# Talking-heads attention with a squared-ReLU FFN: a fixed TensorE order with FFN, AV and transposes as filler, AV heads in paired column tiles, full token tiles, fold on GpSimd

## The chip, the cores and the metric

One core of one Trainium2 chip. Time is device microseconds of one execution. The kernel before takes 1078.01 us (median of four runs beside those of the changed kernel, 1072.89 to 1087.81). A profile is one execution of its own, so its span (1088.0 us for the kernel before, the profile of the slowest of the four runs) differs a little from the median. A "visit" below is one stay of TensorE in a tiling of its array, with entering and leaving: *row tiles* where the two heads of QK read partitions 0 to 63 and 64 to 127, *column tiles* where the two heads of AV write PSUM partitions 0 to 63 and 64 to 127 with 64 stationary columns each.

## The reference, cut to what matters

```python
# q, k, v: (8, 12, 448, 64); w_pre, w_post: (12, 12); w_in: (768, 2048); w_out: (2048, 768)
scores = scale * q @ k.T                                # QK
scores = einsum('bhij,hg->bgij', scores, w_pre)         # pre: mixes the 12 heads
attn   = softmax(scores, axis=-1)                       # exp, row sum, division
attn   = einsum('bhij,hg->bgij', attn, w_post)          # post: mixes the heads again
x      = attn @ v                                       # AV, then tokens x 768
out    = relu(x @ w_in) ** 2 @ w_out                    # first and second FFN matmul
```

The head mixes need the 12 heads of a query on the partition axis. Both kernels handle a chunk of 10 queries, 120 rows of (query, head), 45 chunks to a batch. A chunk goes: QK into PSUM, copy to `stage`, a DMA that relays `stage` (query rows) into `dring` (query and head rows), `pre`, exp on ScalarE with its row sum, reciprocal on VectorE, *fold* (post's matrix scaled by the reciprocals), `post`, copy to `a2t`.

## The kernel before

Each batch's work is a list of tasks with estimates, and a greedy planner decides the order on every engine by start time and priority. AV runs once all 45 chunks of a batch are done. It splits the 448 keys into row blocks of 128, 128, 128 and 64, and takes the two heads of a pair one after the other:

```python
for p in range(NPAIR):
    for kk in range(2):                       # the two heads of a pair
        kh = 2 * p + kk
        for jb in range(NJT):                 # 4 blocks of keys
            nrj = min(128, S - jb * 128)      # 128, 128, 128, 64
            last = eng.matmul(
                psV[kk * 64:kk * 64 + 64, hcol0:hcol0 + ncol],
                vbv[0:nrj, pb, jb, kh, :],            # stationary, 64 columns
                a2t[0:nrj, jb, kh, 0:nch_h * CH],     # moving, 450 columns
                start=(jb == 0), stop=(jb == NJT - 1))
    ...
# first FFN: one PSUM bank (psH), 16 groups of 6 matmuls, relu and square on VectorE
# second FFN: four token tiles a batch (128, 128, 128, 64), 32 matmuls each, in one go
for hh, (f0, fw) in enumerate(FSPL):
    for t16 in range(NFFT):
        last = eng.matmul(psA[0:M, hh, 0:fw], h2t[:, t16, tt*128:tt*128+M],
                          w_out_sb[:, t16, f0:f0+fw], ...)
# fold, on VectorE
i1 = eng.reciprocal(rinv[:, psl, :], rowsum[:, psl, :])
selfsync(DVE, eng, i1)
return eng.tensor_scalar(wk2s[:, ws, :], wk2b[:, :], rinv[:, psl, :], None, op0=ALU.mult)
```

The softmax here doesn't subtract the row's maximum and nothing guards it: scores larger than these inputs give would overflow.

## Time and profile before

| | kernel before |
|---|---|
| median time | 1078.01 us |
| span of the profile | 1088.0 us |
| TensorE busy | 866.5 us (80%) |
| VectorE, ScalarE busy | 495.5 and 435.4 us |
| mean granted TensorE clock | 0.786 |
| from one batch's first post to the next one's (batches 1 to 7) | 119.6 us |

The page's totals, and its strip of 40 equal slices. A digit is the busy share of a slice in tenths; PEclk is the granted clock in tenths of full speed.

```profile
PE 866.5 (80%) x4744; PEld 413.6 (38%) x4744; DVE 495.5 (46%) x1377; ACT 435.4 (40%) x1061; POOL 98.0 (9%) x108
...
PE   1356678897889798788989798888889798848777
...
ACT  0345544634354515643353615543454425430001
...
PEclk9555669895998759995798759996989569965559
```

TensorE is the busiest engine, but much of this time is at half clock. The stage table of the kernel before says when (columns: stretch, its length, busy time and instructions of each engine, granted clock, DMA share, GB/s):

```profile
140.00:160.00 20.00, 14.51 (x59) 5.62 (x59) 7.62 (x19) 7.36 (x18) 0.00 (x0) 0.64 0.23 39
...
460.00:480.00 20.00, 18.88 (x131) 11.85 (x130) 3.86 (x15) 7.67 (x21) 0.00 (x0) 1.00 0.29 81
...
500.00:520.00 20.00, 18.81 (x49) 5.44 (x50) 4.68 (x9) 4.43 (x7) 0.00 (x0) 0.50 0.17 34
...
1000.00:1020.00 20.00, 15.69 (x39) 4.58 (x38) 5.32 (x10) 0.00 (x0) 0.00 (x0) 0.50 0.00 1
```

The four rows are batch 0's attention, a second FFN stage (VectorE and ScalarE have little to do), an AV stage, and the end (batch 7's first FFN). Two of them run at clock 0.50, and in the AV row TensorE is nevertheless busy 18.8 of 20 us.

TensorE's timeline of the kernel before, first a mixed stage at full clock, then AV (start, length, what, how many):

```profile
427.06 0.40 PE L368 MATMUL psA<-ktp,qtp 64*120 64x448 bf16 x2
427.39 0.40 PE L427 MATMUL psP<-dring,wk 120*120 120x448 bf16 x1
427.85 1.31 PE L560 MATMUL psH<-xt,w_in_sb 128*128 128x448 bf16 x6
429.09 0.40 PE L368 MATMUL psA<-ktp,qtp 64*120 64x448 bf16 x2
...
502.23 3.62 PE L514 MATMUL psV<-a2t,vbv 128*64 128x450 bf16 x8
505.78 0.63 PE L368 MATMUL psA<-ktp,qtp 64*120 64x448 bf16 x2
506.57 3.62 PE L514 MATMUL psV<-a2t,vbv 128*64 128x450 bf16 x8 [0.16 <-DVE xt L535]
```

Starts, not lengths, give the cost: a QK pair is recorded with 0.40 us, but the next matmul starts 0.33 us after it. A first-FFN group takes 1.24 us to a following QK and 1.14 us where `pre` follows. An AV group (one pair of heads) lasts 3.62 us, and QK follows after 3.55; the groups recur every 4.34 us.

### The profile page before, as it was taken

The page shows a single profiled execution, that of the slowest core. Times are in us where ns is not written, and L with a number is a line of the kernel's source. Part 1 is how long each engine was busy: PE and PEld are TensorE (multiplying, and loading weights), DVE is VectorE, ACT ScalarE, POOL GpSimd, SP SyncE. Part 2 cuts the span into 40 slices and gives each one's busy share as a digit, 9 for nine tenths or more (in the row PEclk, how much of TensorE's full clock was granted, in tenths as well). Part 3 has the DMA queues.
Part 4 walks back from the last instruction along what each step waited for, and adds up shares of the span by engine and source line. Part 5 has one row for each costly group of instructions (what it writes and reads, how often), then busy time and mean ns, then how long its engine had stood idle before and what let it go on. Part 6 is the DMA issues. An engine that isn't in the chain of part 4 may idle for free.

```text
span 1088.0 us, 13619 instructions
## 1 busy us (share of the span) xinstructions
PE 866.5 (80%) x4744; PEld 413.6 (38%) x4744; DVE 495.5 (46%) x1377; ACT 435.4 (40%) x1061; POOL 98.0 (9%) x108
## 2 busy tenths in 40 slices
PE   1356678897889798788989798888889798848777
PEld 1122323463345424452345424452446234522224
DVE  1134536815573527643582527543763447331320
ACT  0345544634354515643353615543454425430001
POOL 8500201002100201011100200000100000000000
PEclk9555669895998759995798759996989569965559
DMA  9996916329532917348532907331633213220001
GB/s 94 183 204 79 101 32 78 53 65 112 64 55 52 114 22 86 58 84 80 70 55 64 106 16 86 58 80 29 81 49 82 44 36 57 62 48 0 1 0 51
DMA packets 184643, 73.25 MB, mean 67 GB/s; under 512 B 135168, under 2 KB 180224, under 8 KB 184576
## 3 DMA queue, kind: packets, MB, share of 16 engines
q0 software_dynamic: 133408, 22.81, 29.3%
q1 hardware_dynamic: 51168, 49.57, 22.8%
q8 instruction: 38, 0.62, 0.2%
q14 instruction: 29, 0.24, 0.1%
HBM read 45.62 MB, written 11.01 MB: 52 GB/s over the span
## 4 chain that ended last, share of the span: by engine, by line
PE 36%; DVE 13%; ACT 4%; issue 4%; DMA 3%; SPq 0%; DVEq 0%; ACTq 0%
PE psA L607 12%; PE psV L514 10%; PE psH L560 9%; DVE h1t L577 4%; DMA dring<-stage 3%; PE psQ L467 2%; DVE a2t L491 2%; DVE wk2s L455 2%; ACT pring L439 2%; DVE xt L535 2%; PE psP L427 2%; ACT osb L627 1%; DVE rinv L453 1%; PE psA L368 1%; DVE stage L389 1%
## 5 line engine op out<-in xcount | busy, mean ns | idle before, releaser
L439 ACT ACTIVATE pring<-psP 120x448 bf16<-120x448 f32 x360 | 193.8, 541 | 230.7 <-PE psP L427 149.8
L467 PE MATMUL psQ<-wk2s,pring 120*128 120x120 bf16 x1440 | 148.7, 242 | 86.6 <-DVE wk2s L455 70.8
L560 PE MATMUL psH<-xt,w_in_sb 128*128 128x448 bf16 x768 | 187.0, 385 | 27.5 <-DVE h1t L577 18.2
L607 PE MATMUL psA<-w_out_sb,h2t 128*128 128x384 bf16 (+1 forms) x1024 | 179.0, 335 | 10.9 <-ACT osb L627 9.2
L388 ACT ACTIVATE stage<-psA 120x896 bf16<-120x896 f32 (+1 forms) x128 | 117.3, 917 | 139.6 <-PE psA L368 138.3
L427 PE MATMUL psP<-dring,wk 120*120 120x448 bf16 x360 | 148.1, 436 | 30.8 <-DMA dring<-stage 24.9
L467 PEld LDWEIGHTS psQ<-wk2s,pring 120*128 120x128 bf16 x1440 | 105.2, 109 | 158.3 <-ACT pring L439 77.6
L514 PE MATMUL psV<-a2t,vbv 128*64 128x450 bf16 (+1 forms) x384 | 153.6, 524 | 12.5 <-DVE xt L535 11.8
L453 DVE RECIPROCAL rinv<-rowsum 120x1 f32<-120x1 f32 x360 | 57.3, 159 | 226.4 <-ACT pring L439 184.9
L491 DVE CAST a2t<-psQ 128x480 bf16<-128x480 f32 x180 | 117.6, 654 | 70.5 <-PE psQ L467 70.4
L607 PEld LDWEIGHTS psA<-w_out_sb,h2t 128*128 128x128 bf16 (+1 forms) x1024 | 103.1, 103 | 81.8 <-ACT osb L627 14.6
L490 ACT ACTIVATE a2t<-psQ 128x480 bf16<-128x480 f32 x180 | 103.3, 574 | 53.3 <-PE psQ L467 53.2
L368 PE MATMUL psA<-ktp,qtp 64*120 64x448 bf16 (+1 forms) x384 | 99.2, 513 | 24.4 <-ACT stage L388 10.3
L627 ACT ACTIVATE osb<-psA 128x768 f32<-128x768 f32 (+1 forms) x32 | 25.9, 809 | 224.9 <-PE psA L607 224.9
L577 DVE TENSOR_SCALAR h1t<-psH 128x448 bf16<-128x448 f32 x128 | 79.7, 623 | 76.4 <-PE psH L560 74.6
L560 PEld LDWEIGHTS psH<-xt,w_in_sb 128*128 128x128 bf16 x768 | 69.7, 104 | 117.9 <-DVE h1t L577 55.8
L455 DVE TENSOR_SCALAR wk2s<-wk2b,rinv 120x120 bf16<-120x120 bf16 x360 | 98.3, 273 | 12.7
L535 DVE CAST xt<-psV 128x448 bf16<-128x448 f32 x48 | 30.0, 625 | 134.5 <-PE psV L514 134.5
L514 PEld LDWEIGHTS psV<-a2t,vbv 128*64 128x64 bf16 (+1 forms) x384 | 42.8, 135 | 123.6 <-issue 90.6
L427 PEld LDWEIGHTS psP<-dring,wk 120*120 120x120 bf16 x360 | 53.8, 152 | 77.2 <-DMA dring<-stage 34.6
L389 DVE CAST stage<-psA 120x896 bf16<-120x896 f32 (+1 forms) x64 | 69.4, 1084 | 14.6 <-PE psA L368 14.3
L439 ACT ACTIVATION_READ_ACCUMULATOR pring<-psP 120x1 f32 x360 | 72.0, 200 | 0.0
(26 smaller groups left out, 281.2 us busy)
## 6 DMA issues: line engine op xcount, KB each, us to landing
dring<-stage SPq DMA_DIRECT2D x352, 105.0 KB
out_dram<-osb SPq DMA_DIRECT2D x24, 384.0 KB, 2.3
qraw<-in_q_dram POOLq DMA_DIRECT2D x32, 168.0 KB, 6.5
kraw<-in_k_dram POOLq DMA_DIRECT2D x32, 168.0 KB, 6.8
vbv<-in_v_dram POOLq DMA_DIRECT2D x24, 192.0 KB, 6.4
w_in_sb<-in_moe_w_in_dram POOLq DMA_DIRECT2D x1, 3072.0 KB, 19.7
w_out_sb<-in_moe_w_out_dram POOLq DMA_DIRECT2D x1, 3072.0 KB, 40.8
out_dram<-osb SPq DMA_DIRECT2D x8, 192.0 KB, 2.6
```

The source lines that it names most:

```text
L368: last = eng.matmul(psA[0:nr, par, 0:S], qtp[r0:r0 + 64, p, T * IT:T * IT + nr], ktp[r0:r0 + 64, p, 0:S], start=True, stop=True,)
L388: return eng.activation(o, i_, AF.Copy)
L427: return eng.matmul(psP[0:NR, pbank, 0:S], wk1[:, :], dring[:, slot, 0:S], start=True, stop=True)
L439: return eng.activation(pring[:, psl, 0:S], psP[0:NR, pbank, 0:S], AF.Exp, accum_out=rowsum[:, psl, :],)
L455: return eng.tensor_scalar(wk2s[:, ws, :], wk2b[:, :], rinv[:, psl, :], None, op0=ALU.mult)
L467: last = eng.matmul(psQ[0:128, qbank, jb * NR:(jb + 1) * NR], pring[:, psl, jb * 128:jb * 128 + 128], wk2s[:, ws, :], start=True, stop=True,)
L490: return eng.activation(dst, src, AF.Copy)
L491: return eng.tensor_copy(dst, src)
L514: last = eng.matmul(psV[kk * 64:kk * 64 + 64, hcol0:hcol0 + ncol], vbv[0:nrj, pb, jb, kh, :], a2t[0:nrj, jb, kh, 0:nch_h * CH], start=(jb ...
L560: last = eng.matmul(psH[0:128, 0:S], w_in_sb[:, ft, t16 * 128:(t16 + 1) * 128], xt[:, pb, ft, 0:S], start=(ft == 0), stop=(ft == NFT - 1),)
L577: return eng.tensor_scalar(h1t[:, hslot, 0:S], psH[0:128, 0:S], 0.0, None, op0=ALU.max)
L607: last = eng.matmul(psA[0:M, hh, 0:fw], h2t[:, t16, tt * 128:tt * 128 + M], w_out_sb[:, t16, f0:f0 + fw], start=(t16 == 0), stop=(t16 == N ...
```

## The change

The kernel is rewritten around one idea: TensorE's order is fixed by the program, chunk by chunk, and everything that is not the chain of chunks becomes filler in small pieces.

```diff
+        def window(b):                         # filler of batch b's window
+            head = weave(units_AV(b - 1, 1), late_f2, 2)      # AV, second half of batch b-1
+            f1 = units_F1(b - 1, ...)                         # first FFN, 2 pieces of 3 matmuls
+            ts = units_T(b + 1) if b + 1 < B else []          # next batch's transposes
+            body = weave(f1, ts, 2)
+            body += mark(lambda: emit_load_qk(b + 2))
+            body += units_F2(b - 1, ...)                      # second FFN, 4 pieces of 4 matmuls
+            tail = units_AV(b, 0)                             # AV, first half (26 chunks) of batch b
...
+            if 0 <= s + LP < NG:
+                emit_pre(s + LP)                # pre runs 3 chunks ahead of post
...
+                    while openg or queue:       # filler, paced by its share of the work left
+                        if w and owed < w / 2:
+                            break
...
+        emit_load_qk(0); emit_load_v(0); emit_load_w()        # the loads' order in the program
+        for p in range(NP):
+            emit_T(0, p)
+            emit_QK(*qk_order[p])
+        emit_load_qk(1)
```

AV now splits the keys into four blocks of 112 rows, and its two heads alternate; there are two halves of 260 and 188 columns:

```diff
-                                for kk in range(2):
-                                    for jb in range(NJT):
-                                        nrj = min(128, S - jb * 128)
+                for r in range(RJ):             # 4 blocks of 112 keys
+                    for kk in range(2):
+                        r_ = eng.matmul(psF[kk * 64:kk * 64 + 64, bank, 0:n],
+                                        vraw[:, 2 * p + kk, r, :],
+                                        a2t[half][:, r, 2 * p + kk, 0:n], ...)
```

The 64-token rest of an even batch shares a second-FFN tile with that of the odd batch after it (28 full tiles instead of 32). Fold runs on GpSimd, and the squares too, except batch 7's. Evictions go to ScalarE or VectorE as the planner's model finds either free; the transposes are made as half-width tiles (768 instead of 384); q, k and v are loaded in rows of 4 tokens, so with a quarter of the pieces.

## The prediction

> **What bounds the kernel now.** Totals show TensorE busy 866.5 of 1088 us, VectorE 495.5, ScalarE 435.4, mean granted clock 0.786. The stage table (20 us windows) shows three regimes:
> - Opening (to 245 us, when batch 0's FFN ends): from 40 to 160 us TensorE is busy 7 to 15 of each 20 us at clock 0.50 to 0.64; nothing fills the attention's waits.
> - Steady, about 119 us a batch (second FFN matmuls recur at 340, 460, 580). AV alone (500 to 527) runs at clock 0.50 although TensorE is busy 18.8 of 20 us: 64 columns a matmul, the two heads of a pair in sequence. The second matmuls run with ScalarE and VectorE nearly idle; attention after them waits for wk2s and psA.
> - Ending (960 to 1088): batch 7 alone, mostly clock 0.50, each first matmul group waiting for its relu.
>
> So TensorE's order and clock bound the time.
>
> **TensorE at full clock**, start to start in the timeline: first FFN group 1.14 us, second 0.162 us per matmul, pre 0.19, post 0.21 (4 matmuls), QK pair 0.33 plus 0.10 before it. Two concurrent row tiles need 0.19, so entering and leaving costs about 0.24. The Trainium skill (TensorEngine Tiling (Array Packing), Key Properties) says that changing the tiling mode drains TensorE; this agrees.
>
> **What the change does there.**
> - AV: 384 matmuls of 450 columns in sequence (27 us a batch at half clock) become paired column tiles. The skill (TensorE: Matmul & The Clock Gate, Part 3) says such tiles run concurrently; here only QK's row tiles show it. Estimate 7.6 us a batch with switches, at full clock.
> - Second FFN: 28 full tiles for 32, 166 to 146 us.
> - Transposes: 768 half-width for 384; estimate 38 us with switches, some 18 more.
> - FFN, AV and transposes fill between pre, QK and post: TensorE should not idle, the clock stay near 1.0 (mixed windows at 420 to 460 show 1.00).
>
> Sum after, at full clock (estimate): pre 68, post 76, QK 83, AV 61, transposes 38, FFN 146 + 146: about 618 us.
>
> **Other engines.** Fold leaves VectorE (98 us) for GpSimd, as do squares (50) except batch 7's. Evictions split flexibly: from the measured durations at most 460 us each on ScalarE and VectorE, below TensorE. GpSimd: estimate 300 to 350 us, off the path with three chunks of lookahead (some 5 us). Q, k, v loads get four times fewer packets. The relayout DMAs (38 MB) stay, with slack.
>
> **Predicted time.** Opening 25 us until chunks flow; batch 0, limited by ScalarE/VectorE and the weight loads' DMA, about 55; windows 1 to 7 about 80 each (78 of TensorE work plus waits), 560; ending 30. Total about 670 us: steady periods save some 40 each, the opening 85, the ending 95. Range 620 to 745. Faster by over 2%: 0.97; within 2%: 0.02; slower: 0.01.
>
> **What shows it right or wrong.** Mean clock over 0.9; TensorE busy over 90% from 100 us on; period near 80 us; AV matmuls starting in pairs, about 1.3 us per head pair over both halves; batch 0 chunks every 1.2 us; GpSimd not high among TensorE's releasers; ending under 40 us.
>
> **What would make it wrong.** (1) Mode switches cost over 0.24 us, or come more often, with QK, AV and transposes scattered: period 90 or more. (2) Column tiles don't overlap: 7 us a period. (3) Fold late behind squares or DMA issues on GpSimd: posts wait, and the fixed order has no way around. (4) Weight loads crowd the opening's relayouts and the clock stays 0.5: 30 to 50 us. (5) Evictions late, two psF banks serving four stages. If everything overlaps better: 620.

## The result, and the profile after

| | before | after |
|---|---|---|
| median time | 1078.01 us | 721.18 us (720.45 to 723.25, 4 runs) |
| span of the profile | 1088.0 us | 718.5 us |
| TensorE busy | 866.5 us (80%) | 629.5 us (88%) |
| mean granted clock | 0.786 | 0.985 |
| first post of batch 0 | 48.2 us | 64.0 us |
| first post of batch 1 | 170.7 us | 144.5 us |
| batch to batch, batches 1 to 7 | 119.6 us | 75.3 us |
| from batch 7's first post to the end | 199.4 us | 122.3 us |

The ratio is 0.6682 (95% interval 0.6646 to 0.6718). Ratios are the mean time of one kernel's fast runs over that of the other's of the same rounds, so not quite the ratio of the medians quoted. Executions over 1.5% slower than the fastest of the same kernel are left out of the means. Where I compare experiments with the changed kernel, I give medians in us. The kernel before scattered in the later jobs (1046 to 1095 us in the last, where eight of its eleven runs count as slow) and several verdicts against it are marked unclear for that reason; the changed kernel and its variants stay within about 1%.

The page's totals and strip after:

```profile
PE 629.5 (88%) x5576; PEld 368.6 (51%) x5576; DVE 380.7 (53%) x946; ACT 488.9 (68%) x1129; POOL 287.0 (40%) x566
...
PE   3314779987889999999999999999999999999996
...
ACT  4314660897878967788778867887788676866510
```

From the thirteenth slice on (216 us) TensorE is full. The stage table after, cut at the windows of the batches (a window runs from a batch's first post to the next one's); columns as before:

```profile
0.00:64.00 64.00, 14.97 (x137) 7.69 (x138) 7.71 (x12) 16.70 (x25) 15.39 (x31) 1.00 1.02 173
64.00:144.00 80.00, 66.83 (x558) 40.81 (x556) 47.89 (x116) 48.07 (x118) 27.48 (x61) 0.91 0.38 74
144.00:208.00 64.00, 52.27 (x578) 33.40 (x578) 44.56 (x116) 53.42 (x137) 28.20 (x67) 0.95 0.63 122
...
288.00:362.00 74.00, 73.89 (x669) 41.52 (x665) 45.37 (x111) 60.61 (x140) 36.15 (x68) 1.00 0.57 109
362.00:442.00 80.00, 78.24 (x691) 44.13 (x685) 45.71 (x111) 62.26 (x142) 36.14 (x68) 1.00 0.53 109
...
682.00:718.00 36.00, 29.31 (x252) 18.97 (x250) 12.22 (x35) 3.84 (x11) 2.75 (x5) 0.99 0.12 45
```

Windows alternate between 74 and 80 us, because even batches bring three second-FFN tiles and odd ones four; they run in the window of the next batch. TensorE is busy all but 2 us of them, at clock 1.00. The first 64 us are another matter: TensorE is busy 15 us. Their clock of 1.00 is not a measurement: the trace records no change of clock before 75.5 us, and the views put 1.00 where nothing is recorded. By the lengths of its matmuls (0.58 us for `post` up to 74.8 us, 0.39 at 75.5) TensorE ran at half clock until then.

TensorE's timeline after, in a full window (the parts answer to the lines shown of before):

```profile
337.46 0.38 PE L489 MATMUL psQ<-wk2s,pring 120*128 120x120 bf16 x4
337.76 0.63 PE L521 MATMUL psF<-a2t,vraw 112*64 112x260 bf16 x8
338.33 0.40 PE L444 MATMUL psP<-dring,wk 120*120 120x448 bf16 x1
...
342.42 0.40 PE L377 MATMUL psA<-ktp,qtp 64*120 64x448 bf16 x2
342.75 0.38 PE L489 MATMUL psQ<-wk2s,pring 120*128 120x120 bf16 x4
342.97 0.35 PE L444 MATMUL psP<-dring,wk 120*120 120x448 bf16 x1
```

An AV group of 260 columns takes 0.57 us to the next start, plus some 0.09 before it (post alone takes 0.21, here 0.30); with the 188-column half that is about 1.2 us a pair of heads instead of 4.34. And the timeline of the opening:

```profile
39.58 0.63 PE L377 MATMUL psA<-ktp,qtp 64*120 64x448 bf16 x2
41.13 0.63 PE L444 MATMUL psP<-dring,wk 120*120 120x448 bf16 x1 [0.92 <-DMA dring<-stage]
63.08 0.59 PE L336 MATMUL psF<-ident,qraw 112*64 112x112 bf16 x8 [21.32 <-DMA kraw<-in_k_dram]
63.45 0.59 PE L336 MATMUL psF<-ident,kraw 112*64 112x112 bf16 x8
63.97 0.58 PE L489 MATMUL psQ<-wk2s,pring 120*128 120x120 bf16 x4
```

Four chunks have been through `pre` and exp by 42 us, but the first `post` comes at 64 us. Ahead of it, in the fixed order, stand the transposes of batch **1**, and they wait 21.32 us for batch 1's k. That load was issued at 24.4 us; the whole of `w_in` and `w_out` had been issued from the same queue at 14 us. The list of DMA issues has the k loads of one head pair at 4.1 us to landing (median) and this one at 38.6.

### The profile page after: what moved, and what is told of

Its sections match the earlier page's. It is cut to its first block, busy times and chain, and to the rows that moved or that the text cites. A ratio compares the mean times of both kernels' runs of the same rounds, so it can differ in the third digit from the quotient of the medians.

```text
span 718.5 us, 14744 instructions
## 1 busy us (share of the span) xinstructions
PE 629.5 (88%) x5576; PEld 368.6 (51%) x5576; DVE 380.7 (53%) x946; ACT 488.9 (68%) x1129; POOL 287.0 (40%) x566
## 4 chain that ended last, share of the span: by engine, by line
PE 81%; DMA 7%; ACT 4%; DVE 4%; POOL 2%; issue 1%; SPq 0%; POOLq 0%
PE psF L625 21%; PE psF L562 20%; PE psQ L489 13%; PE psP L444 9%; PE psA L377 9%; PE psF L521 6%; DMA kraw<-in_k_dram 6%; PE psF L336 4%; DMA dring<-stage 2%; ACT pring L454 1%; DVE a2t L220 1%; ACT stage L219 1%; POOL h2t L597 1%; DVE qtp L220 1%; ACT a2t L219 1%
## 5 line engine op out<-in xcount | busy, mean ns | idle before, releaser
L469 POOL TENSOR_SCALAR wk2s<-wk2b,rinv 120x120 bf16<-120x120 bf16 x360 | 131.0, 365 | 305.2 <-DVE rinv L463 302.3
L220 DVE CAST a2t<-psQ 112x480 bf16<-112x480 f32 x221 | 144.5, 656 | 99.5 <-PE psQ L489 95.6
L562 PE MATMUL psF<-xt,w_in_sb 128*128 128x448 bf16 (+2 forms) x960 | 187.0, 316 | 5.1 <-DVE ktp L220 3.2
L625 PE MATMUL psF<-w_out_sb,h2t 128*128 128x384 bf16 x896 | 177.2, 325 | 9.0 <-POOL h2t L597 7.4
L597 POOL TENSOR_TENSOR h2t<-h1t 128x448 bf16<-128x448 bf16 (+2 forms) x128 | 107.3, 839 | 37.0 <-DVE h1t L588 17.6
L625 PEld LDWEIGHTS psF<-w_out_sb,h2t 128*128 128x128 bf16 x896 | 82.0, 98 | 54.1 <-POOL h2t L597 9.3
L562 PEld LDWEIGHTS psF<-xt,w_in_sb 128*128 128x128 bf16 x960 | 84.1, 99 | 47.8 <-DVE ktp L220 5.6
L377 PE MATMUL psA<-ktp,qtp 64*120 64x448 bf16 (+1 forms) x384 | 80.5, 416 | 26.3 <-ACT stage L219 13.6
L219 ACT ACTIVATE a2t<-psQ 112x480 bf16<-112x480 f32 x139 | 80.0, 575 | 28.8 <-PE psQ L489 24.9
L377 PEld LDWEIGHTS psA<-ktp,qtp 64*120 64x120 bf16 (+1 forms) x384 | 25.0, 127 | 81.8 <-issue 32.0
L521 PE MATMUL psF<-a2t,vraw 112*64 112x260 bf16 (+1 forms) x768 | 53.5, 264 | 1.7 <-DVE a2t L220 0.7
L588 DVE TENSOR_SCALAR h1t<-psF 128x448 bf16<-128x448 f32 (+2 forms) x89 | 43.8, 492 | 10.6 <-PE psF L562 9.0
```

Source lines behind the costliest of these rows:

```text
L219: return eng.activation(o, i_, AF.Copy)
L220: return eng.tensor_copy(o, i_)
L377: r_ = eng.matmul(psA[0:nr, par, 0:S], qtp[r0:r0 + 64, pb, p, T * IT:T * IT + nr], ktp[r0:r0 + 64, pb, p, 0:S], start=True, stop=True,)
L469: return eng.tensor_scalar(wk2s[:, ws, :], wk2b[:, :, :].rearrange("p a b -> p (a b)"), rinv[:, ps, :], 1.0, op0=ALU.mult, op1=ALU.mult)
L521: r_ = eng.matmul(psF[kk * 64:kk * 64 + 64, bank, 0:n], vraw[:, 2 * p + kk, r, :], a2t[half][:, r, 2 * p + kk, 0:n], start=(r == 0), stop= ...
L562: r_ = eng.matmul(psF[:, bank, 0:n], w_in_sb[:, ft, t16 * 128:(t16 + 1) * 128], xt[:, ft, c0:c1], start=(ft == 0), stop=(ft == NFT - 1),)
```

## The experiments

Twelve kernels were run; all gave correct results. Those named b change the kernel before, the others the changed kernel (721.18 us).

### e1: weights after batch 1's loads, first try

```diff
         emit_load_v(0)
-        emit_load_w()
         ...
         emit_load_qk(1)
+        emit_load_w()
```

> The changed kernel (721 us) with one edit: the FFN weight loads are issued after batch 1's q and k loads instead of before them. Theory A (the opening lost to the load order: TensorE stands 21 us at batch 1's first transpose because its k tile is queued behind 12.6 MB of weights): that wait goes, chunk 0's post starts near 40 us instead of 64, and the run takes 700 to 708 us; not the whole 21 us, because the relayouts of batch 0 now compete with the weights for longer. Rival (the opening is bound by TensorE's own chain of transposes, evictions and half clock, the load wait only hides it): under 5 us gained.

Measured 721.61 us (716.67 to 724.08), with the same wait of 21.5 us. This decides nothing: the instruction lists of all engines, GpSimd's included, turned out to be identical to those of the changed kernel. So e1 is a second sample of it, in another job. The planner orders GpSimd's tasks by readiness and priority, and the weights were ready earlier and ranked higher. Moving a line in a program whose order is made by a planner is not an edit; look at the instruction list of the engine before running.

### e2: batch 1's transposes later in the order, loads unchanged

```diff
             ts = units_T(b + 1) if b + 1 < B else []
-            body = weave(f1, ts, 2)
+            if b == 0: late_t.extend(ts + mark(lambda: emit_load_qk(2)))
+            else:      body = weave(f1, ts, 2)
...
+            if b == 0 and c == 14:
+                queue, owed = late_t, 0.0
```

> The changed kernel with the loads in their old order, but batch 1's transposes put into TensorE's order from chunk 14 of batch 0 on instead of ahead of chunk 0's post. Theory A with the fixed order as its second half (the late load stops TensorE only because the order puts its transposes first): posts start near 42 us instead of 64 while the weights still load, time 700 to 708 us. If the load alone mattered and the order did not: no gain, TensorE waits for the same DMA later.

Measured 707.75 us (705.49 to 709.12), 13 us less. The first post comes at 41.5 us, and its timeline reads:

```profile
41.12 0.63 PE L444 MATMUL psP<-dring,wk 120*120 120x448 bf16 x1 [0.91 <-DMA dring<-stage]
41.54 0.61 PE L489 MATMUL psQ<-wk2s,pring 120*128 120x120 bf16 x4
43.23 0.63 PE L444 MATMUL psP<-dring,wk 120*120 120x448 bf16 x1 [1.08 <-DMA dring<-stage]
...
70.78 0.59 PE L336 MATMUL psF<-ident,qraw 112*64 112x112 bf16 x8 [6.01 <-DMA kraw<-in_k_dram]
```

So the wait came of the late load and the order together: with the order alone changed, the wait ahead of the first post is gone. The 22 us gained at the first post shrink to 13 because the chunks now come every 2.1 us, at the pace at which their relayouts pass beside the weight loads (each `pre` waits for its DMA), and chunk 14's transposes still wait 6 us for k.

### e8: the loads' order really changed

```diff
-            last["w_in"] = plan.add("ldwin", POOL, fn_in, [qk_tasks[(0, H - 1)]], ..., -300.0, ...)
+            last["w_in"] = plan.add("ldwin", POOL, fn_in, [last["T"]], ..., 600.0, ...)
             # the same for w_out; emit_load_w() after emit_load_qk(1) as in e1
```

> e1 repeated with the order really changed: the edit of e1 left GpSimd's queue as it was, because its own planner sorts loads by priority and readiness; here the weight loads wait for the last transpose of batch 0 and rank behind batch 1's q and k. TensorE's order is that of the changed kernel. Theory A (load order): the 21 us wait for batch 1's k tile shrinks to under 3 us, posts start near 41 us, but the relayouts now run beside the weights until about 95 us at 2.1 us a chunk, and the first FFN group may wait for w_in a little: 703 to 712 us. Rival (own chain and half clock): over 716 us.

Measured 710.74 us (707.82 to 711.82). The wait for k is gone, the first post comes at 42.9 us, and again only half of the gain stays. In e2 and in e8 alike, TensorE reaches AV of batch 0's first 26 chunks at 92.2 us, against 104.3 in the changed kernel. Two opposite cures end at the same moment, which would fit a limit in the bytes of the DMA queues, but no run isolates it. The stage table of e8 shows them full up to 70 us (last two columns: DMA share, which counts packet time and passes 1.0 here, and GB/s):

```profile
40.00:50.00 10.00, 5.50 (x60) 3.41 (x60) 3.75 (x7) 2.77 (x6) 0.73 (x2) 1.00 1.08 221
50.00:60.00 10.00, 8.01 (x73) 4.88 (x74) 4.46 (x10) 7.19 (x14) 2.65 (x4) 1.00 1.13 222
60.00:70.00 10.00, 5.82 (x31) 2.77 (x29) 5.09 (x14) 5.05 (x13) 2.29 (x7) 1.00 1.21 219
```

From 70 to 90 us the share is 0.77. In e2 it falls to 0.69 and 0.28 from 60 to 80 us, and the 6 us wait for k lies there; so the queues are not full all the way to 92 us in either run.

The Trainium skill says that DMAs from the SP, ACT and POOL queues all run on the same 16 DMA engines and interleave (Trainium Kernel Development and Optimization, Key Constraints). This agrees: in e2 a chunk's relayout from the SP queue passes every 2.1 us beside the weights from the POOL queue; once `w_out` has landed at 55.4 us, chunks come every 1.25 us on average until the wait at 64.4 us.

### e3: AV's two heads one after the other

```diff
-                for r in range(RJ):
-                    for kk in range(2):
+                for kk in range(2):
+                    for r in range(RJ):
```

> The changed kernel with the two heads of a pair run one after the other in AV (all four row groups of one head, then of the other), nothing else changed. Column tiles overlap theory: the matmuls no longer start in pairs, AV costs 0.73 us more per head pair over both halves, 48 pairs, 35 us in all: 750 to 760 us, clock still over 0.95 because other work surrounds AV. Rival 1 (tiles don't overlap, it was the weaving that saved the time): no change. Rival 2 (unpaired AV pulls the clock to half as it did in the kernel before): 800 us or more.

Measured 722.05 us (715.34 to 723.59): no change, where I expected 35 us more. Rival 1, no overlap at all, is not the reason either, for an AV group still takes 0.57 to 0.58 us, and eight matmuls of 260 columns in sequence would take 8 x 0.11 us (0.11 is the step between starts within one head):

```profile
332.03 0.64 PE L521 MATMUL psF<-a2t,vraw 112*64 112x260 bf16 x8
332.61 0.40 PE L444 MATMUL psP<-dring,wk 120*120 120x448 bf16 x1
```

The single starts in that group, from the trace, are 332.033, .047, .168, .182, .279, .292, .390 and .403: still in pairs, 13 to 14 ns apart (4 ns in the changed kernel). So the two column tiles overlap **even though the program gives four matmuls of one head first**. The trace doesn't name the tile of a matmul, but two of one head, which add into the same PSUM cells, are 0.11 us apart; the partner in each pair must be the other head's.

Then why did the heads not overlap in the kernel before, in the same order? Its single starts in one group are 502.234, 502.613, 502.987, 503.499, 504.009, 504.386, 504.761 and 505.272. Steps are 0.375 us, but 0.51 into and out of the fourth matmul, the one with only 64 rows. A new theory: the 64-row block, a different tiling in the middle, keeps the heads apart. The next two runs test it on the kernel before.

### b2: the kernel before with four blocks of 112 keys, heads in sequence

```diff
-                    nrj = min(128, S - jt * 128)
-                    off = b * H * S * D + jt * 128 * D
+                    nrj = S // NJT                                   # 112, in the load of v
+                    off = b * H * S * D + jt * nrj * D
-                                pring[:, psl, jb * 128:jb * 128 + 128],
+                                pring[:, psl, jb * 112:jb * 112 + 128],
-                                        nrj = min(128, S - jb * 128)
+                                        nrj = S // NJT               # in AV
```

> The kernel before, with only the split of the 448 keys changed: four blocks of 112 rows instead of 128, 128, 128 and 64, in the loads of v, post's slices and AV; the two heads still in sequence. Theory U: without the 64-row block no tiling change stands between the heads and they overlap by themselves, as they did in e3: an AV group takes 1.9 to 2.2 us instead of 3.6 at the half clock, 48 groups, 70 to 80 us less: 995 to 1015 us. Rival (heads in sequence do not overlap in this kernel; e3 overlapped for another reason): no change, 1070 to 1085 us.

Measured 1016.3 us (1014.63 to 1020.26), just above the range, and 43 us under the median of the three fast runs of the kernel before in that job (1059.75). The ratio is 0.9634 (0.9534 to 0.9733), unclear for their scatter; the timeline is clear. The group has become:

```profile
482.58 1.72 PE L514 MATMUL psV<-a2t,vbv 112*64 112x450 bf16 x8
485.04 1.72 PE L514 MATMUL psV<-a2t,vbv 112*64 112x450 bf16 x8 [0.18 <-DVE xt L535]
```

The period of the groups falls from 4.34 to 2.46 us without any change of order, and that of the batches from 119.6 to 110.0 us.

### b1: the kernel before with the heads alternating, blocks unchanged

```diff
-                                for kk in range(2):
-                                    kh = 2 * p + kk
-                                    for jb in range(NJT):
-                                        nrj = min(128, S - jb * 128)
+                                for jb in range(NJT):
+                                    nrj = min(128, S - jb * 128)
+                                    for kk in range(2):
+                                        kh = 2 * p + kk
```

> The kernel before, with only AV's loop order changed: row block outside, the two heads inside, so that heads alternate as in the changed kernel. Row blocks stay 128, 128, 128 and 64. Theory U (what keeps the heads apart in the kernel before is the 64-row block, which changes the tiling, not the order): with the order changed too, the three 128-row blocks start in pairs and the 64-row pair once more, so an AV group takes about 2.4 us instead of 3.6 at the half clock, 48 groups, 55 to 60 us: 1015 to 1030 us. Rival (order alone decides and nothing else): groups of about 1.9 us.

Measured 1026.28 us (1022.65 to 1030.98), inside the range (ratio 0.9725, 0.9619 to 0.9831, unclear for the same reason), but the group takes 1.85 us, not the 2.4 I expected:

```profile
487.68 1.85 PE L514 MATMUL psV<-a2t,vbv 128*64 128x450 bf16 x8
```

So either edit is enough alone: alternate the heads, and the 64-row pair comes last and costs 0.13 us against b2; or cut even blocks, and the order no longer matters. What separates the heads in the kernel before is the combination, the odd block standing between them. In both runs an AV matmul still lasts 0.58 us, the half-clock length, and the granted clock from 480 to 500 us is 0.50: pairing did not lift the clock of a stage that runs by itself with gaps.

### e4: filler in one block

```diff
-                        if w and owed < w / 2:
+                        if False:
                             break
```

> The changed kernel with the pacing taken out: each window's filler (AV, first and second FFN matmuls, transposes) is emitted in one block at the start of its window, then the 45 chunks of attention follow. Theory (interleaving is what hides the chunks' chain of exp, reciprocal, fold and evictions): a window becomes about 45 us of dense FFN with ScalarE idle plus 45 to 60 us of attention with TensorE under 70% busy, 95 to 105 us instead of 77: 830 to 900 us. Rival (the gain came from cheaper TensorE work alone, order is secondary): under 750 us.

Measured 872.09 us (867.67 to 874.77), 151 us more than the changed kernel, inside the range. The same TensorE work falls apart into stages again. Two rows of the stage table of this run, the block of filler and the 45 chunks after it:

```profile
218.00:274.00 56.00, 50.05 (x375) 26.43 (x376) 13.30 (x20) 14.54 (x33) 20.54 (x26) 0.96 0.41 73
274.00:323.00 49.00, 38.92 (x322) 22.24 (x320) 36.39 (x90) 41.96 (x114) 15.58 (x43) 0.90 0.42 92
```

In the first ScalarE is busy 14.5 of 56 us; in the second it is busy 42 of 49, nearly the limit, and TensorE 39. The windows become 94 to 106 us. The two stages load different engines, and interleaving is what lets them share the time.

### e5: fold back on VectorE

```diff
-            t_fold = add("fold%d_%d" % (b, c), POOL, fn_fold, ..., {POOL: (350.0, 450.0)}, ...)
+            t_fold = add("fold%d_%d" % (b, c), DVE, fn_fold, ..., {DVE: (200.0, 280.0)}, ...)
```

> The changed kernel with fold back on VectorE (0.27 us each, 98 us in all). Theory (TensorE's work bounds the steady windows, 100% busy; VectorE has room at 53% busy): within 1%, 715 to 728 us, VectorE about 65% busy. Rival (moving fold off VectorE is part of the gain): over 735 us.

Measured 721.24 us (719.9 to 722.65): the same. VectorE rises to 62% busy and has room. Moving fold to GpSimd is harmless and buys nothing here.

```profile
PE 628.8 (88%) x5576; PEld 367.1 (51%) x5576; DVE 448.1 (62%) x1263; ACT 500.3 (70%) x1172; POOL 157.7 (22%) x206
```

### e6: every QK pair twice

```diff
-                for par in range(2):
+                for par in (0, 1, 0, 1):
```

> The changed kernel with every QK pair issued twice in a row (the second overwrites the first with the same values). It prices QK without entering and leaving its row tiles. Prediction's reading (two concurrent row tiles 0.19 us, plus 0.24 us once per visit): 192 times 0.19 us, about 35 us, of which some in the unfilled opening: 745 to 760 us. Rival (the pair itself costs 0.43 us, there is no cost of changing the tiling): 83 us more, 795 to 805 us.

Measured 747.63 us (744.37 to 752.07), 26 us more, and the visit in its timeline is now 0.52 us to the next start, against 0.33:

```profile
313.35 0.59 PE L377 MATMUL psA<-ktp,qtp 64*120 64x448 bf16 x4
313.87 0.38 PE L489 MATMUL psQ<-wk2s,pring 120*128 120x120 bf16 x4
```

A second pair costs 0.19 us, what two concurrent row tiles of 448 columns should. The remaining 0.14, and the 0.10 seen before the visit, are paid once a visit. The total is under 192 x 0.19 = 36 us because window 0, which was not full, did not grow (77 us, where e3, e5 and the changed kernel have 75 to 80); windows 2 to 6 grew by 4.5 us each for 24 pairs (24 x 0.19 = 4.6).

### e7: no shared token tiles

```diff
-            return 64 if b % 2 == 0 else 0        # hbase
+            return 0
-            return list(range(4 if b % 2 else 3)) # tiles_of
+            return list(range(4))
             # and 64 rows instead of 128 in tile 3's matmuls, copy and store
```

> The changed kernel with the 64-token tails of two batches no longer sharing a tile: 32 second-FFN tiles instead of 28. Four more tiles of 32 matmuls at 0.162 us are 20.8 us of TensorE in windows where it is 100% busy: 738 to 746 us. Rival (a half-width tile costs half, because only 64 columns are loaded): 4 tiles less half of 8, no change.

Measured 746.12 us (742.94 to 748.94), 25 us more, just above the range. A tile of 64 tokens costs TensorE no less than one of 128, and here even more: the windows that had three tiles went from 74.1 to 81.9 us, and those that had four, of which one is now of 64 tokens, from 79.9 to 81.8. The timeline shows a piece of 128 tokens and one of 64:

```profile
281.11 0.82 PE L624 MATMUL psF<-w_out_sb,h2t 128*128 128x384 bf16 x4
281.76 0.35 PE L444 MATMUL psP<-dring,wk 120*120 120x448 bf16 x1
...
292.30 0.84 PE L624 MATMUL psF<-w_out_sb,h2t 128*64 128x384 bf16 x4
293.07 0.40 PE L444 MATMUL psP<-dring,wk 120*120 120x448 bf16 x1
```

The piece of 64 takes 0.77 us to the next start, against 0.65, and in the medians what stands before it takes 0.09 to 0.14 us longer. That is 0.2 to 0.25 us a piece, 8 pieces a tile: the 2 us that both kinds of window grew beyond a full tile. With 64 columns the piece is a visit of column tiles like AV's, and pays for it.

### e9 and e10: what the experiments point to

e9 is e2 with batch 1's transposes from chunk 18 on, and with the opening's transposes one head pair ahead of their QK. e10 adds AV two head pairs at a time.

```diff
-        for p in range(NP):
-            emit_T(0, p)
-            emit_QK(*qk_order[p])
+        emit_T(0, 0)
+        for p in range(NP):
+            if p + 1 < NP:
+                emit_T(0, p + 1)
+            emit_QK(*qk_order[p])
...
-            return [[(RJ * (n / 2.4 + 7.0), (lambda p=p: emit_AV(b, half, p)))]
-                    for p in range(NP)]
+            return [[(2 * RJ * (n / 2.4 + 7.0),                                    # e10
+                      (lambda p=p: (emit_AV(b, half, p), emit_AV(b, half, p + 1))))]
+                    for p in range(0, NP, 2)]
```

> e2 (708 us) with two further edits in the opening: batch 1's transposes from chunk 18 on instead of 14, since at 14 TensorE still waited 6 us for their k tile, and the first six transposes run one head pair ahead of their QK, so that evictions overlap the next transposes. Theory (the opening is load order, then the DMA queue shared by weights and relayouts, then the chain of transposes): the first relayout goes out near 20 us instead of 27, the 6 us wait goes: 695 to 702 us. Rival (the opening is now bound by the bytes of weights and relayouts alone): 705 to 708 us.

> e9 with AV emitted two head pairs at a time, so that TensorE enters and leaves the column tiles 48 times instead of 96. If a visit costs 0.2 to 0.24 us beyond the work, 48 visits less are 9 to 11 us in windows that are 100% busy; some is lost where the next FFN group waits for a psF bank: 6 to 11 us below e9. Rival (leaving column tiles costs nothing, the drain seen belongs to row tiles): no difference.

e9 measured 702.55 us (701.27 to 706.05, 6 runs), 5 us under e2, which ran in another job, and a hair above the range. Windows 2 to 7 take 474.1 us in both profiles, so the 5 us are of the stretch before them. The first relayout is issued at 19.6 us instead of 26.5, but the first chunk's `pre` then waits 7.18 us for it and runs at 29.1 us instead of 34.8; AV of the first half begins at 88.7 us instead of 92.2. Most of the 7 us won at the front go to waiting for the DMA queues, which is what the rival said.

e10 measured 698.49 us (696.22 to 699.8, 6 runs), 4 us under e9 in the same job and with no overlap of the runs, but less than the 6 to 11 expected. Two head pairs together take 1.01 us to the next start where two single groups take 2 x 0.57, and one entry of about 0.09 is saved as well:

```profile
321.13 1.08 PE L521 MATMUL psF<-a2t,vraw 112*64 112x260 bf16 x16
322.14 0.40 PE L377 MATMUL psA<-ktp,qtp 64*120 64x448 bf16 x2
```

That is some 0.2 us a visit, 10 us in 48 visits saved. By first posts, windows 2 to 7 took 474.1 us in e9 and 467.3 in e10, 7 us less, and window 0 took 1 us less, but window 1 took 5 us more (63.8 to 68.8); why is open. e10 is the fastest version: its ratio to the kernel before is 0.6614 (0.6558 to 0.6671; unclear because of the scatter of the kernel before in that job), and it is 3% under the changed kernel by the medians, of different jobs.

## Why the prediction was right or wrong

The time was predicted as 670 us with a range of 620 to 745, and measured as 721.18. The range holds, the centre is 7% low. By parts, from the first posts:

| part | predicted | measured | difference |
|---|---|---|---|
| opening, until chunks flow | 25 | 64.0 | +39 |
| window 0 | 55 | 80.5 | +25 |
| window 1 | 80 | 63.9 | -16 |
| windows 2 to 7 | 6 x 80 | 474.1 | -6 |
| ending | 30 | 36 | +6 |

- **Right: TensorE's order and clock bound the time, not VectorE.** TensorE is busy all but 2 us of the full windows, at clock 1.00 (predicted over 0.9; the mean is given as 0.985, and is about 0.93 by my estimate with the first 75.5 us at half clock), and 95% of the time from 100 us on (predicted over 90%). e4, the same work without interleaving, is 151 us slower; e5, which gives VectorE its fold back, is not slower. Of the other parts, the shared tiles are worth 25 us (e7), and even AV blocks some 43 us in the kernel before (b2). These do not add up to the 357 us gained, and no run separates what the higher clock is worth by itself.
- **Right: the sum of TensorE's work by start-to-start times.** 78 us a window was the estimate; windows 2 to 7 take 74 to 80, and 86 for the last with its extra FFN work. Each unit priced in the timeline of before held: e6 confirms the 0.19 + 0.24 us of a QK visit, and e7 that a tile costs at least its 32 matmuls. AV took about 1.2 us a head pair (1.3 predicted), a transpose visit about 0.6 us (0.8 predicted).
- **Right: GpSimd is off the path.** It is busy 287 us (300 to 350 estimated), and TensorE waits for it little. From the list of waits after (who waited for whom: us in total, times, longest):

```profile
PE psF L336 <- DMA kraw<-in_k_dram: 26.9, 2, 21.3
...
PE psF L625 <- POOL h2t L597: 7.4, 5, 1.6
```

- **Half wrong, its size right: "the two heads of a pair in sequence" as the cause of AV's cost.** Paired AV came out as predicted, but e3 shows that the order of the heads is not what does it in the changed kernel: heads in sequence overlap as well. b1 and b2 show that in the kernel before the 64-row block between the heads kept them apart, and that either even blocks or alternating heads cure it. The prediction did not look at the 112-row split as part of the change at all.
- **Wrong: the clock of AV.** I read the half clock of the AV stage as a matter of 64 columns a matmul. b1 and b2 pair the heads and still run AV at the half-clock length (0.58 us). In the changed kernel and in e3, where AV stands among other matmuls, it runs at full clock. What in that company raises it, no run isolates.
- **Wrong in size: "Opening 25 us until chunks flow".** It measured 64. The named risk was weight loads that crowd the relayouts; that is there, but the largest piece is one I had not seen: batch 1's q and k queue behind the weights (2 x 768 x 2048 values, 12.6 MB in fp32), and the fixed order puts batch 1's transposes ahead of the first post. e2 (order) and e8 (loads) each bring the first post to 41.5 and 42.9 us. Of the 39 us, 21 to 22 are this; the rest, some 17, is the chain of transposes and QK, at half clock, up to the first relayout at 26.6 us, and the relayouts beside the weights. The same two runs show that the end gains only 10 to 13 us of the 22: both reach batch 0's AV at 92.2 us. That the DMA engines hold them there is argued, not shown.
- **Wrong: "batch 0, limited by ScalarE/VectorE and the weight loads' DMA, about 55".** Window 0 took 80.5 us, 1.8 us a chunk instead of 1.2. ScalarE and VectorE are busy only 48 us each of it, TensorE 67. Part of this is a shift: half of batch 0's AV and first-FFN work already runs in window 0 (AV from 104.3 us on), and window 1 is shorter by 16 us. Both windows together are 9 us over; that they come so close is partly this shift.
- **Wrong in size: "the opening 85".** The gain up to batch 1's first post is 26 us (170.7 to 144.5), by the two points above. The ending saved 77 us for 95 (199.4 to 122.3 from batch 7's first post), the steady periods 44 each for 40.
- **Small:** the ending took 36 us for 30. No run isolates it.

## What to carry to other kernels

Where an engine's order is fixed, look for the first task in it that needs a late load, and check the queue in front of that load; the cheapest cure may be to move the task, not the load. Price an engine's work by start-to-start times of the trace at a known clock and add the visits to other tilings as an item of their own: this sum was good to a few per cent (480 us predicted for windows 2 to 7, 474 measured). When two tiles should overlap and don't, look at the shapes between them as well as at the order.

## What the Trainium skill lacked or had wrong

- *TensorE: Matmul & The Clock Gate*, Part 3 ("What overlaps and what doesn't"), says that matmuls start and end strictly in program order. In e3 four matmuls of one column tile stand ahead of four of the other, and their starts still come in pairs 13 to 14 ns apart; the last of the eight starts 0.37 us after the first, where starts in program order would need at least six steps of 0.11 us. The trace doesn't name the tiles, so the pairing is inferred from the step of 0.11 us within one head.
- *TensorEngine Tiling (Array Packing)*, Key Properties, says that changing the tiling mode drains TensorE, without a size. Here a QK visit costs 0.24 us beyond its work (e6), a visit of column tiles about 0.2 us (e10, and a 64-token piece in e7). The page doesn't spell out that a block of other height inside a run of column tiles counts as such a change and keeps neighbouring tiles apart: steps of 0.51 us instead of 0.375 around the 64-row block, and 3.62 us a group instead of 1.72 without it (b2).
- *TensorE: Matmul & The Clock Gate*, Part 1 (HAM trace caveats), warns that the clock events of a trace are unreliable. In the changed kernel the recorded changes agree with the lengths of the matmuls (half clock from 79.0 to 89.2 us, where `post` lasts 0.58 us, against 0.37 just before and after), but none is recorded before 75.5 us: the views show 1.00 there, while `post` lasts 0.58 us. The mean of 0.985 is too high by that.
- *GPSIMD Engine Reference*, section 3.1, gives about 2.6 cycles an element for a two-input elementwise operation, measured in fp32; it has no figure for bf16. The bf16 squares here took 498 ns for 188 elements and 932 ns for 448: 1.67 ns an element, 2.0 cycles of the page's 1.2 GHz.
- *SBUF — State Buffer* says in its note on cachelines that bf16 data may be strided by up to 8 elements for free. The q transposes are now copied from PSUM to SBUF with a step of 4 bf16 elements at the destination: 1169 ns on ScalarE, where the k copy of the same size without a step takes 543, and 1157 on VectorE, where the kernel before's plain q copy took 384. No page has the cost of such a write, and no run here isolates the step from the copy's other shape. TensorE waits six times 1.8 us for these copies and the k copies behind them, all in the opening.
